# Dummy matmuls from the first microsecond, other banks for the last unit of the first group, and a few casts on other engines

## The chip, the cores and the metric

One Trainium2 chip, one of its cores. The metric is the device time of one execution in microseconds (us). The kernel before takes 340.81 us (median of 3 runs, 340.48 to 345.62). A difference counts as faster or slower from 2% on. A run is called slow when it is over 1.5% above the fastest of the same kernel (345.62 is one); fast runs are compared with fast runs.

## The reference, cut to what matters

```python
# retention: q, k, v of (8 batches, 8 heads, 576 positions, 64)
scores = scale * q @ k^T
ret = scores * Dmat          # Dmat = gamma_h ** (i - j) for i >= j, else 0
x = (ret @ v) -> (4608 tokens, 512)
# feed-forward with ELU
h = x @ w_in                 # 512 -> 2048
g = where(h > 0, h, exp(min(h, 0)) - 1)
out = g @ w_out              # 2048 -> 512
```

## The kernel before

The 4608 tokens go through the feed-forward in nine groups of 512. A group needs the attention output of some "units" (256 positions by four heads; unit 3 is the last that the first group waits for). For each unit VectorE and GpSimd scale q and k to bf16, TensorE transposes both, makes the scores, the running state (k times v) and the values (masked scores times v, plus q times the carried state), and ScalarE copies the result out of PSUM. GpSimd then writes the running state as a bf16 tile for TensorE; such a write is called a "state put" below. Meanwhile the weights arrive in fp32 by DMA and are cast to bf16. PSUM has three banks for `ps_h`, one for `ps_m`, two for the scores (`ps_s`), two for the values (`ps_x`).

The parts that the change touches (cuts are marked):

```python
    def warm(n, d=None):                       # dummy matmuls
        d = ps_s.tile([P, 2, 512], FP32, name="warm", tag="sc")[:, 0] if d is None else d
        for _ in range(n):
            mm(d, ident, zero, start=True, stop=True)

    def last_of_start(u):                      # unit 3, in two halves of two heads
        ...
        new_x()                                # the same two banks as unit 2's values
        both = [None]
        for hl in range(2):
            # VectorE: mask half hl of the scores
            if hl == 0:
                prefix_end(u)
                both.append([ps_h.tile([P, 512], FP32, name="o2", tag="ph") for _ in range(2)])
            values(u, (hl,), both[hl])
            inter(u, (hl,), both[hl])
            put_x(u, (hl,), both[hl], ("ss", "sv")[hl])
            warm(1, both[1][1] if hl == 0 else None)

    ...
    cast(0, "v", None)
    turn_pe(0)
    cast(1, "v", None)
    for u in range(FT - 1):
        scores(u)
        cast_v(u, "s")
        ...                                    # values of the unit before, states of this one
        if u == 2:
            cast_w(0)                          # two weight casts on GpSimd
            cast_v(3, "s")                     # unit 3's v on ScalarE
        ...
        masks(u)
        turn_pe(u + 1, "vs" if u == 2 else "ss")
        ...                                    # states of unit 3, sums, state puts, warm(1)
        if u == 1:
            cast_q(3, nc.vector)
            cast_q(3, nc.gpsimd, 1, (0,))      # unit 3's k: half on GpSimd,
            cast_q(3, nc.vector, 1, (1,))      # half on VectorE
    cast_w(1)
    scores(3)
    ...                                        # values of unit 2
    last_of_start(3)
    ...
    for ft in range(8):
        ffn1(0, ft, relu=ft % 2 == 1)          # four matmuls of 128x512, Exp (and Relu), one or two VectorE passes
    for ft in range(8):
        ffn1(0, 8 + ft, relu=ft % 2 == 1)
        ffn2(0, 0, [ft])
        ffn2(0, 1, [ft], ps_x, "x0")
```

## Time and profile before

| | before |
|---|---|
| time | 340.81 us (340.48 to 345.62) |
| profiled execution | 344.11 us, span 342.4 |
| first feed-forward matmul starts | 22.33 us |
| first copy of an output tile starts | 45.83 us |

The page gives each engine's busy share in 40 slices of the span (9 is 90% or more), and the TensorE clock that the throttle granted, in tenths:

```profile
PE   3889986678667899999999999999999999999995
PEclk9999999989899999999999999999999999999999
```

TensorE is busy for 90% or more of each slice from the 15th to the last but one. The first slices hold the start, and the clock row shows 9 there, although the matmuls run at half speed.

### The profile page before, as it was taken

To read this page: it belongs to the slowest core of one execution; us is meant where nothing else is said; L and a number is where in the kernel's file an instruction comes from. 1 tells how busy PE (TensorE), PEld (TensorE's weight loads), DVE (VectorE), ACT (ScalarE), POOL (GpSimd) and SP (SyncE) were. 2 spreads that over 40 slices of the span, in tenths; PEclk is the share of its full clock that TensorE was granted. 3 is DMA by queue.
4 is the path that set the end of the run, shared out by engine and by line. 5 is a ranking of instruction groups with operands and counts; after the bars stand their busy time and mean duration, and the time that the engine had idled before them with its cause. 6 is when DMAs were issued, how large, how long until landed. Compare 5 with 4: busy or idle time off the path is not lost.

```text
span 342.4 us, 7823 instructions
## 1 busy us (share of the span) xinstructions
PE 307.1 (90%) x3039; PEld 157.1 (46%) x3080; DVE 213.0 (62%) x379; ACT 178.8 (52%) x364; POOL 179.3 (52%) x315
## 2 busy tenths in 40 slices
PE   3889986678667899999999999999999999999995
PEld 1543434345444445444454544554454444444342
DVE  4838724566568998667676676677677565455500
ACT  3627612546244477655555565565556655555511
POOL 5789453555989479364565658556755120000100
PEclk9999999989899999999999999999999999999999
DMA  7999999203999979975259875978422001000021
GB/s 213 319 358 387 264 306 299 70 2 107 157 279 237 263 156 192 189 171 164 86 121 249 169 185 126 241 158 207 93 56 61 32 33 61 32 32 32 31 94 61
DMA packets 100293, 53.86 MB, mean 157 GB/s; under 512 B 44448, under 2 KB 93600, under 8 KB 100256
## 3 DMA queue, kind: packets, MB, share of 16 engines
q1 hardware_dynamic: 97696, 44.97, 55.5%
q0 software_dynamic: 2560, 8.39, 7.8%
q8 instruction: 24, 0.39, 0.5%
q14 instruction: 13, 0.11, 0.1%
HBM read 36.70 MB, written 9.44 MB: 135 GB/s over the span
## 4 chain that ended last, share of the span: by engine, by line
PE 78%; DVE 5%; DMA 5%; ACT 5%; POOL 3%; issue 3%; SPq 1%; DVEq 0%; ACTq 0%; POOLq 0%
PE ph L66 34%; PE pm L66 34%; PE x L66 5%; PE sc L66 3%; DMA qkT<-qkn 3%; DVE em L475 3%; DMA rqk<-in_k_dram 2%; POOL qkn L191 1%; DVE g L482 1%; ACT xt L343 1%; ACT ph L473 1%; ACT ot L492 1%; DVE g L480 1%; ACT e L471 1%; ACT qkT L240 1%
## 5 line engine op out<-in xcount | busy, mean ns | idle before, releaser
L66 PE MATMUL ph<-xt,w_in_sb 128*128 128x512 bf16 (+2 forms) x612 | 149.5, 366 | 10.4 <-DVE g L482 6.8
L66 PE MATMUL pm<-w_out_sb,g 128*128 128x512 bf16 x564 | 144.1, 380 | 2.9 <-ACT ot L492 1.7
L471 ACT ACTIVATE e<-ph 128x512 f32<-128x512 f32 (+2 forms) x152 | 87.3, 574 | 97.6 <-PE ph L66 79.7
L66 PEld LDWEIGHTS <-w_in_sb 128*128 128x128 bf16 x640 | 60.7, 100 | 72.4 <-issue 14.1
L66 PEld LDWEIGHTS <-g 128*128 128x128 bf16 x576 | 55.8, 98 | 69.6 <-issue 7.3
L480 DVE SCALAR_TENSOR_TENSOR g<-e,ph 128x512 bf16<-128x512 f32 (+2 forms) x80 | 50.2, 632 | 49.9 <-ACT ph L473 49.6
L475 DVE TENSOR_SCALAR em<-e 128x512 bf16<-128x512 f32 (+2 forms) x76 | 47.5, 625 | 32.2 <-ACT e L471 32.2
L495 POOL DMA_DIRECT2D out_dram<-ot x32 | 18.3, 573 | 81.5 <-ACT ot L492 81.5
L482 DVE SCALAR_TENSOR_TENSOR g<-ph,em 128x512 bf16<-128x512 f32 (+2 forms) x80 | 50.7, 637 | 3.4
L473 ACT ACTIVATE ph<-ph 128x512 f32<-128x512 f32 (+2 forms) x76 | 43.3, 570 | 0.0
L290 DVE TENSOR_TENSOR pt<-sc,mask 128x1024 bf16<-128x1024 f32 x31 | 37.7, 1217 | 6.8 <-PE sc L66 6.8
L191 POOL TENSOR_TENSOR qkn<-rqk,gk 128x256 bf16<-128x256 f32 x63 | 37.8, 618 | 3.6 <-DMA rqk<-in_k_dram 3.5
L343 ACT CAST xt<-x 128x256 bf16<-128x256 f32 (+1 forms) x72 | 24.2, 415 | 26.2 <-PE x L66 26.1
L492 ACT COPY ot<-pm 128x512 f32<-128x512 f32 x36 | 21.1, 589 | 20.1 <-PE pm L66 20.1
L191 POOL TENSOR_TENSOR qkn<-rqk,gq 128x256 bf16<-128x256 f32 x52 | 31.2, 620 | 0.1
L370 POOL TENSOR_TENSOR s_mid_146<-mid,diag 128x256 bf16<-128x256 f32 x16 | 9.7, 606 | 30.2 <-DVE mid L381 19.3
L370 POOL TENSOR_TENSOR s_mid_147<-mid,diag 128x256 bf16<-128x256 f32 x16 | 9.7, 609 | 28.7 <-DVE mid L381 14.4
L66 PE MATMUL sc<-qkT 64*64 64x128 bf16 (+1 forms) x576 | 16.8, 229 | 4.6 <-DMA qkT<-qkn 3.3
L217 POOL CAST vn<-rv 128x512 bf16<-128x512 f32 x27 | 17.9, 663 | 0.0
L239 PE MATMUL ptr<-ident,qkn 128*128 128x128 bf16 x64 | 8.5, 269 | 8.3 <-DVE qkn L191 6.1
L66 PEld LDWEIGHTS <-qkT 64*64 64x64 bf16 x576 | 10.5, 112 | 10.5 <-DMA qkT<-qkn 3.6
L66 PE MATMUL x<-pt,vn 64*64 64x128 bf16 x504 | 14.2, 227 | 0.5 <-ACT xt L343 0.5
(79 smaller groups left out, 183.2 us busy)
## 6 DMA issues: line engine op xcount, KB each, us to landing
rqk<-in_q_dram SPq DMA_DIRECT2D x32, 256.0 KB, 4.8
rqk<-in_k_dram SPq DMA_DIRECT2D x32, 256.0 KB, 4.6
rv<-in_v_dram SPq DMA_DIRECT2D x32, 256.0 KB, 4.9
out_dram<-ot POOLq DMA_DIRECT2D x32, 256.0 KB, 3.8
rqk<-in_moe_w_in_dram SPq DMA_DIRECT2D x16, 256.0 KB, 6.0
rqk<-in_moe_w_out_dram SPq DMA_DIRECT2D x16, 256.0 KB, 5.4
rqt<-in_q_dram SPq DMA_DIRECT2D x8, 128.0 KB, 4.4
rqt<-in_k_dram SPq DMA_DIRECT2D x8, 128.0 KB, 3.9
```

The costliest lines, as they stand in the source:

```text
L66: pin(nc.tensor.matmul(*a, **kw))
L191: pin(eng.tensor_tensor(natt[u][0][:, i, e], x[:, e], g[:, e], ALU.mult))
L290: pin(nc.vector.tensor_tensor(pt.rearrange("p i h n -> p (i h) n"), sc.rearrange("p i (h n) -> p (i h) n", h=2), mask.rearrange("p k e r - ...
L343: pin(engines[eng[c]](dst, src[:, :, :, a // 2 : (a + n) // 2]))
L370: pin(eng.tensor_tensor(dst.rearrange("p h (j d) -> p h j d", j=2), src.unsqueeze(2).to_broadcast([P, 2, 2, D]), diag.unsqueeze(1).unsquee ...
L471: pin(nc.scalar.activation(e[:, :m], ph[:, :m], AF.Exp))
L473: pin(nc.scalar.activation(ph[:, :m], ph[:, :m], AF.Relu))
L475: pin(nc.vector.tensor_scalar_add(em[:, :m], e[:, :m], -1.0))
L480: pin(nc.vector.scalar_tensor_tensor(dst, e[:, c], -1.0, ph[:, c], ALU.add, ALU.min))
L482: pin(nc.vector.scalar_tensor_tensor(dst, ph[:, c], 0.0, em[:, c], ALU.max, ALU.min))
L492: pin(nc.scalar.copy(ot, pm))
L495: pin(store.dma_start(out[i0 : i0 + P, :], ot))
```

## The change

The intent: keep TensorE busy from the start so that its clock is full when the feed-forward begins, and shorten the road to the first feed-forward matmul. The dummies use only the `zero` tile, so that they need not wait for the identity. Unit 3's values go into the banks that hold the states of units 3 and 2, so that they need not wait for unit 2's values to be copied out. Unit 3's k is now all on GpSimd, its v on GpSimd instead of ScalarE, and the first weight cast is on ScalarE.

```diff
     def warm(n, d=None):
-        d = ps_s.tile([P, 2, 512], FP32, name="warm", tag="sc")[:, 0] if d is None else d
+        d = xps[1] if d is None else d
         for _ in range(n):
-            mm(d, ident, zero, start=True, stop=True)
+            mm(d, zero[:, :P], zero, start=True, stop=True)
...
-    def last_of_start(u):
+    def last_of_start(u, banks):
...
-        new_x()
-        both = [None]
         for hl in range(2):
             ...
-            if hl == 0:
-                prefix_end(u)
-                both.append([ps_h.tile(...) for _ in range(2)])
-            values(u, (hl,), both[hl])
-            inter(u, (hl,), both[hl])
-            put_x(u, (hl,), both[hl], ("ss", "sv")[hl])
-            warm(1, both[1][1] if hl == 0 else None)
+            values(u, (hl,), banks[hl])
+            inter(u, (hl,), banks[hl])
+            put_x(u, (hl,), banks[hl], ("ss", "sv")[hl])
...
+    new_x()
+    warm(7)
     cast(0, "v", None)
-    turn_pe(0)
+    turn_pe(0, between=2)          # two dummies between the q and the k transposes
+    warm(2)
...
+        if u == 0:
+            ...                    # as before, and at its end
+            warm(2, st[1])
+        if u == 1:
+            ...
+            cast_q(3, nc.vector)
+            cast_q(3, nc.gpsimd, 1)
+            cast_v(3, "p")
+            warm(3, st[1])
+    cast_w(0, "s ")                # the first weight on ScalarE
+    masks(2)
+    turn_pe(3, "vs")
+    st3 = [ps_h.tile([P, TG], FP32, name="st", tag="ph") for _ in range(2)]
+    state(3, st3)
+    ...                            # the sums and puts of units 2 and 3, all before unit 3's masks
+    cast_w(0, " p")                # the second on GpSimd
     scores(3)
     ...
-    last_of_start(3)
-    prefix_end(2)
+    cast_w(1)
+    last_of_start(3, (st3, st))
```

More of the change, by code (lines that the diff above doesn't have):

```diff
@@ L151, in load_w, with cast_w @@
             pin(nc.sync.dma_start(staged[k][:, h], src))
-    def cast_w(k):
+    def cast_w(k, eng="pp"):
         for h, src, dst in weights(k):
-            pin(nc.gpsimd.tensor_copy(dst, staged[k][:, h]))
-        staged.pop(k)
+            if eng[h] != " ":
+                pin(engines[eng[h]](dst, staged[k][:, h]))
     rawt, natt, trt, ptt, score_ps, total = {}, {}, {}, {}, {}, {}
@@ L230, in turn, with turn_pe @@
             pin(nc.sync.dma_start_transpose(trt[u], flat(u)))
-    def turn_pe(u, eng="vs"):
+    def turn_pe(u, eng="vs", between=0):
         n = turn_tile(u)
         for i in range(2):
+            if i and between:
+                warm(between)
             if i * 4 < n:
@@ L413, in last_of_start @@
             ))
-            if hl == 0:
-                prefix_end(u)
-                both.append([ps_h.tile([P, 512], FP32, name="o2", tag="ph") for _ in range(2)])
-            values(u, (hl,), both[hl])
-            inter(u, (hl,), both[hl])
-            put_x(u, (hl,), both[hl], ("ss", "sv")[hl])
-            warm(1, both[1][1] if hl == 0 else None)
+            values(u, (hl,), banks[hl])
+            inter(u, (hl,), banks[hl])
+            put_x(u, (hl,), banks[hl], ("ss", "sv")[hl])
         drop(u)
@@ L531 @@
             drop(u - 1)
-        state(u, [ps_m.tile([P, TG], FP32, name="st", tag="pm"), ps_h.tile([P, TG], FP32, name="st", tag="ph")])
-        if u == 2:
-            cast_w(0)
-            cast_v(3, "s")
+        st = [ps_m.tile([P, TG], FP32, name="st", tag="pm"), ps_h.tile([P, TG], FP32, name="st", tag="ph")]
+        state(u, st)
+        if u == 0:
+            masks(0)
+            turn_pe(1, "ss")
+            prefix_mid(0)
+            prefix_end(0)
+            put_mid(0)
+            put_end(0)
+            cast(2, "v", None)
+            warm(2, st[1])
         if u == 1:
             cast(3, None, None)
-        masks(u)
-        turn_pe(u + 1, "vs" if u == 2 else "ss")
-        if u == 2:
-            state(3, [ps_h.tile([P, TG], FP32, name="st", tag="ph") for _ in range(2)])
-        prefix_mid(u)
-        put_mid(u)
-        if u == 2:
-            prefix_mid(3)
-            put_mid(3)
-        else:
-            prefix_end(u)
-            put_end(u)
-            warm(1)
-        if u == 0:
-            cast(2, "v", None)
-        if u == 1:
-            cast_q(3, nc.vector)
-            cast_q(3, nc.gpsimd, 1, (0,))
-            cast_q(3, nc.vector, 1, (1,))
-    cast_w(1)
+            masks(1)
+            turn_pe(2, "ss")
+            prefix_mid(1)
+            prefix_end(1)
+            put_mid(1)
+            put_end(1)
+            cast_q(3, nc.vector)
+            cast_q(3, nc.gpsimd, 1)
[6 more added lines that the diff above has]
+    state(3, st3)
+    prefix_mid(2)
+    put_mid(2)
+    prefix_end(2)
+    prefix_mid(3)
+    put_mid(3)
+    prefix_end(3)
+    cast_w(0, " p")
     scores(3)
```

## The prediction

> **What bounds the kernel now.** The page first: TensorE is busy in 90% of the span and carries 78% of the chain that ended last, but the 40 slices show its first ten partly below that (3889986678). The change touches only what stands before the first feed-forward group, so I read the chain of waits there, then the timeline, engine by engine. Chain (start, length, what):
>
> ```profile
> 18.22 1.17 PE x L66 x20
> 19.39 0.44 ACT xt L343
> 19.87 1.06 PE x L66 x9
> 20.93 0.36 issue
> 21.29 0.31 PE o_523 L66 x2
> ...
> 22.05 0.43 PE warm L66
> 22.47 3.44 PE ph L66 x8
> 25.96 0.47 issue
> ...
> 29.05 2.89 PE ph L66 x12
> ```
>
> Two things are to be seen. Unit 3 (the last of the first group) waits from 19.39 to 19.87 for ScalarE to copy unit 2 out of the same two banks, and only then do its matmuls, its copies and a dummy run, so the feed-forward starts at 22.33. And the first eight feed-forward matmuls take 3.44 us, 0.43 each. The same instruction is twice as fast later (TensorE's timeline; start, time, count):
>
> ```profile
> 22.33 5.30 PE L66 MATMUL ph<-xt,w_in_sb 128*128 128x512 bf16 x16
> ...
> 36.78 0.59 PE L66 MATMUL pm<-w_out_sb,g 128*128 128x512 bf16 x2
> 37.21 1.03 PE L66 MATMUL ph<-xt,w_in_sb 128*128 128x512 bf16 x4
> 38.08 0.59 PE L66 MATMUL pm<-w_out_sb,g 128*128 128x512 bf16 x2
> ```
>
> From 36.78 to 38.08 six matmuls start, 0.216 us each. The weight loads step by 0.43 us until 25.70 and by about 0.215 after it. So TensorE is at half speed for its first 25.8 us. The view of the granted clock prints 1.00 for these stretches, for its records begin only with the first change; the cadence is the evidence, not that column.
>
> What feeds unit 3 (timeline of all engines):
>
> ```profile
> 13.59 0.92 DVE L191 TENSOR_TENSOR qkn<-rqk,gq 128x256 bf16<-128x256 f32 x2 [0.56 <-DMA rqk<-in_q_dram]
> 14.52 0.61 POOL L191 TENSOR_TENSOR qkn<-rqk,gk 128x256 bf16<-128x256 f32 x1 [0.62 <-DMA rqk<-in_k_dram]
> 14.54 0.87 DVE L191 TENSOR_TENSOR qkn<-rqk,gk 128x256 bf16<-128x256 f32 x1
> 15.34 1.21 DVE L290 TENSOR_TENSOR pt<-sc,mask 128x1024 bf16<-128x1024 f32 x1
> 15.66 1.04 PE L239 MATMUL ptr<-ident,qkn 128*128 128x128 bf16 x8
> 16.73 0.59 ACT L240 COPY qkT<-ptr 128x512 bf16<-128x512 bf16 x1
> 18.26 0.69 DVE L410 TENSOR_TENSOR pt<-sc,mask 128x512 bf16<-128x512 f32 x1 [0.17 <-PE sc L66]
> 19.07 0.68 DVE L410 TENSOR_TENSOR pt<-sc,mask 128x512 bf16<-128x512 f32 x1
> ```
>
> Unit 3's q and k come from DMAs that land at about 13.6 and 14.5; the DMA engines are full from 4 us on (share 1.0 or more), and the change leaves their order alone. So nothing can move unit 3's k before 14.5. After that, 7.8 us pass until the feed-forward starts: casts, transposes, copy, states, scores, masks, values, copies.
>
> **What the Trainium skill says.** "TensorE: Matmul & The Clock Gate", Part 1 (The HAM clock gate): the array starts at half clock and is released after a busy window of about 3.4 us; the window is free-running, so the moment varies by run; a window of idle brings the half clock back. The trace agrees: 0.43 against 0.216 us, and full speed comes at 25.77, one window after dense 512-wide matmuls began at 22.33. It also shows that the small matmuls before did not do it: in 12.1 to 15.5 us I work out that columns streamed in some 74% of the time (a quarter of the window being transposes), and the clock stayed half. Part 4 (PE-mode transpose) states that transposes do not count as busy in the same way, which fits. Re-throttling is seen too: TensorE idles 1.97 us before 73.38, and from 73.56 the granted clock is 0.5 for 3.4 us; I work out 37% streaming in the window before. "Back-to-back issue gap" there gives 512/1.2 GHz = 427 ns cold for one dummy, as measured here.
>
> **The change, part by part.**
>
> *Dummies.* 16 added (7 at the start, 2+2 around unit 0's transposes, 2 after unit 0, 3 after unit 1), 4 removed. They now read only the zero tile, ready at 1.21 us, so seven run from about 1.25 to 1.25 + 7 x 0.427 = 4.24 us, where TensorE idled until 4.31 anyway: free. The next two fill 5.0 to 5.85 and push the k transposes from 5.39 by about 0.45, but the second k half is ready only at 5.96; cost 0 to 0.3 us in a stretch where units 1 to 3 wait for DMA. The others sit before scores that wait for ScalarE's copy. Their worth is the clock. Dense cover of a 3.4 us window is between 60% and 88% by phase, 80% or more with the transposes. The lowest window that I see release the clock is near 86 to 100%, the highest that fails is 74%, of which 25% transposes. I give 75% that the clock is full before 9 us, then some risk of losing it in 9 to 19 us, where warm matmuls stream only 30 to 50% of a window.
>
> *Road to the feed-forward, warm.* k of unit 3 lands at 14.45. Both halves are now on GpSimd, 14.52 + 2 x 0.61 = 15.74 (before 15.41, shared with VectorE): +0.3. VectorE, rid of its k half, does unit 2's mask at 14.51 instead of 15.34 and is free at 16.15 for copies and sums. Transposes end about 16.0 (before 16.70), ScalarE's copy at 16.05 to 16.65 (before 17.32); ScalarE's weight cast (0.6, about 15.3 to 15.9) just fits before it. GpSimd casts unit 3's v in 15.74 to 16.40 (0.66), so its states end near 16.9. VectorE's four sums take 0.39 each, 16.15 to 17.6; then unit 3's masks at 17.6 and 18.25, ending 18.3 and 18.95 (before 18.95 and 19.75). With its own banks the wait of 0.54 and the dummies fall away: values and carried part about 0.35, copies 0.45, twice, the second ending near 19.65. GpSimd is the rival on this road: the state puts until 17.86, then weights 1, 2, 3 at 0.57 each, until 19.57. So the start is about 19.8, against 22.33: **2.5 us**. Cold, the same road ends near 21.0 (scores, values and dummies at half speed): 1.3 us.
>
> *First eight feed-forward tiles.* Before, tile 0 starts at 22.33 and tile 8 at 31.96: 9.63. Warm, TensorE needs 8 x 4 x 0.216 = 6.9, but VectorE needs 4 x (0.61 + 0.69) + 4 x 0.69 = 8.0, and a tile waits for the product three tiles earlier (three banks). Walking that through, tile 8 starts after 7.4: **2.2 us**. Not the 8 x 0.215 = 1.7 of the cold matmuls alone, since the three banks then stay filled. Weights: tile 4 needs cast 7 (about 21.8; tile at 23.5), tile 8 needs cast 11 (25.3; 27.2), and the first w_out tile (28.2) would hold its matmuls some 0.2 us. **-0.2**.
>
> *After that* TensorE is the bound at 1.29 us a tile in both, and the order is the same to the end, so I expect the gain to be carried whole.
>
> Sum, warm: 2.5 + 2.2 - 0.2 = 4.5, so 336.3. Cold throughout: 1.3, so 339.5. Weighted 0.75 to 0.25: 337.1. The profiled run had its window begin just as the feed-forward did; an average run gets the clock up to a window later, so the change is worth about 0.5 more: **336.6**.
>
> **Rivals.**
> 1. *The clock is not released early, or lost again before the feed-forward.* For: no window before 22 us released it in the old kernel, and windows at 37% lost it. Against: windows at 38% and 41% near 53 to 63 us kept it. Time: 338 to 339.5.
> 2. *GpSimd's casts take over as the bound.* It does 0.57 to 0.66 us pieces without a pause from 14.5 to 38. For: weight 3 is done 0.2 us before I need it. Against: one cast moved to ScalarE and the weights land (w3 at 17.25) well before. If it slips by 0.6, 337.2.
> 3. *A transfer or a later wait eats the gain.* w_out's last half lands at 38.1 whatever happens; but it is needed only near 41. The inputs for the next group land at 39 to 48 and are used from 48 on, so 4.5 us earlier still holds. Time if lost: 340.
> 4. *More gain.* The start cannot come before about 19.2 (DMA at 14.45 and the chain behind it), the first eight tiles cannot gain over 2.5; with a late clock in the old kernel's runs 6.5 in all: 334.3.
>
> **Range and chances.** 334.4 to 339.6 holds the warm case with an error of 1.5 to 2 us and the cold case. Faster by over 2% needs under 334.0, a gain of 6.8, more than rival 4 can collect: 0.06. Slower by over 2% has no mechanism: 0.01. Runs with a lost clock window (the old kernel's 345.62, the profiled 344.11) are of another state and are not the comparison.
>
> **What would show it.** Dummies from about 1.25 us; the dummies after unit 0 at 0.216 us a piece and not 0.43; unit 3's masks ending near 18.9 and its values following without ScalarE's wait; the first feed-forward matmul at 19.8 (19.3 to 20.5); tile 8 starting 7.4 us after it; about 4.5 us less at the first output copy (45.83 before). Wrong if the matmuls at 20 us still step by 0.43, if GpSimd's weight cast ends the wait before the first feed-forward matmul, or if the first output copy is early and the end is not.

## The result, and the profile after

The changed kernel takes 337.03 us (median of 4 runs, 335.59 to 338.07); the old one beside it takes 340.84 (4 runs). The ratio is 0.9889, with a 95% interval of 0.9843 to 0.9935: the same within 2%, and clear of no change. A ratio is the mean time of one kernel's fast runs over that of the other's fast runs of the same rounds, so it is not quite the ratio of the medians. The profiled run of the changed kernel was its fastest, 335.59 us, with a span of 333.9. Its two rows of the slices:

```profile
PE   7789985767679999999999999999999999999995
PEclk9999999999979999999999999999999999999999
```

In the first slice TensorE is now busy for 7 tenths instead of 3; that is the dummies. The timeline of all engines, start and length in us, of the lines that answer to those shown of before:

```profile
1.27 3.17 PE L66 MATMUL x<-zero 128*128 128x512 bf16 x7 [1.27 <-DVE zero L75]
...
14.65 1.21 DVE L292 TENSOR_TENSOR pt<-sc,mask 128x1024 bf16<-128x1024 f32 x1
14.74 1.19 POOL L191 TENSOR_TENSOR qkn<-rqk,gk 128x256 bf16<-128x256 f32 x2 [0.62 <-DMA rqk<-in_k_dram]
...
15.66 0.63 ACT L156 CAST w_in_sb<-rqk 128x512 bf16<-128x512 f32 x1
...
16.31 0.59 ACT L242 COPY qkT<-ptr 128x512 bf16<-128x512 bf16 x1
...
17.89 1.28 DVE L410 TENSOR_TENSOR pt<-sc,mask 128x512 bf16<-128x512 f32 x2
...
18.62 0.31 PE L66 MATMUL st<-pt,vn 64*64 64x128 bf16 x8 [0.46 <-DVE pt L410]
...
19.58 2.75 PE L66 MATMUL ph<-xt,w_in_sb 128*128 128x512 bf16 x11
...
20.20 1.85 PEld L66 LDWEIGHTS <-w_in_sb 128*128 128x128 bf16 x10 [0.30 <-POOL w_in_sb L156]
```

The dummies start at 1.27. Unit 3's k lands late as before (GpSimd starts at 14.74, waiting for the DMA), VectorE masks unit 2 at 14.65 instead of 15.34, unit 3's values wait for VectorE's mask and no longer for ScalarE, and the first feed-forward matmul starts at 19.58 instead of 22.33. Eleven of them span 2.75 us, so they run at the full clock; the record of the clock has the release at 4.74. The weight loads stop 0.30 us before 20.20 for a weight cast of GpSimd, but the matmuls keep their step of 0.216 us through it (twelve slots from 19.58 to 22.17, with one record missing), so the start of the feed-forward doesn't wait for it. The chain of waits (start, length, what) says what holds the stretch after it:

```profile
17.72 0.61 POOL s_mid_147 L372
18.33 4.10 POOL w_in_sb L156 x7
22.43 0.58 POOL s_end_149 L372
23.01 0.57 POOL s_end_151 L372
23.58 5.04 POOL w_in_sb L156 x8
28.62 0.57 POOL w_out_sb L156
29.19 0.04 issue
29.23 0.59 PE pm L66 x2
...
42.17 0.60 ACT ot L488
```

Before, this stretch was TensorE, at half clock, and VectorE. Now the chain names GpSimd's state puts and casts, one after the other, until the first matmul with w_out at 29.23. The first output copy starts at 42.17, against 45.83: 3.66 us earlier.

The next table follows the difference to the end, from the timelines of several profiles. The last column has the stretches of half clock that the record of the clock shows after the first release and before 110 us, by their start; each is one window of 3.41 us, except where a number of windows is given.

| profile | first ff matmul | first output copy | from there to the 4th | 4th to 6th | 6th to last | half clock from |
|---|---|---|---|---|---|---|
| before (slow run) | 22.33 | 45.83 | 15.28 | 47.22 | 230.23 | 73.6, 90.6 |
| before, again (state unknown) | 22.70 | 46.21 | 16.34 | 48.15 | 227.11 | 57.4, 91.5, 108.6 |
| changed | 19.58 | 42.17 | 15.29 | 46.18 | 226.38 | 93.5 |
| changed, again | 19.84 | 42.40 | 16.58 | 48.86 | 226.39 | 9.7, 54.1, 95.1 (3) |
| no dummies (e2) | 20.62 | 43.87 | 15.28 | 45.52 | 226.60 | 91.6 |
| more dummies (e6) | 19.26 | 41.74 | 15.29 | 46.69 | 226.38 | 69.4, 93.3 |

The gain is made before the first output copy and is not given back. What scatters the time afterwards lies almost all before 110 us: the stretch from the first to the fourth output copy takes 1.1 to 1.3 us more when a half-clock window falls in it (16.34 and 16.58 against 15.28). From the sixth copy on the changed kernels need 226.4 to 226.6 us in every profile of this table. Part of the scatter of the first column is the landing of unit 3's k, which differs from profile to profile: 14.45 in the old kernel's first, 14.77 in its second, 14.67 in the changed one's, 14.28 in e6's. The old kernel's slow profile has 230.23 there; it holds a single stop of TensorE of 3.69 us before 112.85 that the other profile of that kernel lacks (112.85 is after its sixth copy, at 108.33), so its span of 342.4 is not to be held against 333.9.

### The profile page after: what moved, and what is told of

It is laid out like the page before. It is cut to its first block, busy times and chain, and to the rows that moved or that the text cites.

```text
span 333.9 us, 7841 instructions
## 1 busy us (share of the span) xinstructions
PE 303.7 (91%) x3049; PEld 154.4 (46%) x3092; DVE 208.1 (62%) x378; ACT 178.8 (54%) x364; POOL 180.7 (54%) x316
## 4 chain that ended last, share of the span: by engine, by line
PE 76%; POOL 9%; DVE 4%; DMA 3%; ACT 3%; issue 2%; SPq 0%; POOLq 0%; ACTq 0%; DVEq 0%
PE pm L66 35%; PE ph L66 32%; PE x L66 5%; PE sc L66 3%; POOL qkn L191 3%; POOL w_in_sb L156 3%; DMA qkT<-qkn 2%; DMA rqk<-in_q_dram 2%; DVE pt L292 1%; DVE g L478 1%; ACT ot L488 1%; DVE em L471 1%; POOL s_mid_147 L372 1%; ACT xt L345 1%; ACT ph L469 1%
## 5 line engine op out<-in xcount | busy, mean ns | idle before, releaser
L66 PE MATMUL ph<-xt,w_in_sb 128*128 128x512 bf16 (+2 forms) x611 | 145.7, 358 | 6.6 <-DVE g L478 3.7
L66 PEld LDWEIGHTS <-w_in_sb 128*128 128x128 bf16 x640 | 59.3, 98 | 66.2 <-issue 8.0
L471 DVE TENSOR_SCALAR em<-e 128x512 bf16<-128x512 f32 (+2 forms) x76 | 43.2, 569 | 31.4 <-ACT e L467 31.4
L191 POOL TENSOR_TENSOR qkn<-rqk,gk 128x256 bf16<-128x256 f32 x64 | 38.5, 621 | 3.5 <-DMA rqk<-in_k_dram 3.5
L66 PE MATMUL sc<-qkT 64*64 64x128 bf16 (+1 forms) x576 | 16.1, 222 | 3.2 <-DMA qkT<-qkn 2.8
L217 POOL CAST vn<-rv 128x512 bf16<-128x512 f32 x28 | 18.8, 671 | 0.0
L66 PE MATMUL x<-pt,vn 64*64 64x128 bf16 x496 | 13.1, 221 | 0.0
L241 PE MATMUL ptr<-ident,qkn 128*128 128x128 bf16 x64 | 7.3, 227 | 5.7 <-POOL qkn L191 2.3
```

Source lines behind the costliest of these rows:

```text
L66: pin(nc.tensor.matmul(*a, **kw))
L191: pin(eng.tensor_tensor(natt[u][0][:, i, e], x[:, e], g[:, e], ALU.mult))
L217: pin(engines[eng](natt[u][1], rawt[u][1]))
L471: pin(nc.vector.tensor_scalar_add(em[:, :m], e[:, :m], -1.0))
```

## The experiments

Eleven runs, of ten kernels and the old one again, were made. All were correct. The old kernel took 339.3 to 340.3 us (medians) beside them. The first two calls ran on one chip, the third (e7, e8, e9) on another, so means are compared within the first two or within the third, and ratios across them.

### e1: the dummies alone

The old kernel with the new `warm`, `new_x(); warm(7)`, `between=2`, `warm(2)`, `warm(2, st[1])` and `warm(3, st[1])`; nothing else of the change.

> The old kernel with the new dummies alone (seven from 1.25 us on, two and two around unit 0's transposes, two after unit 0, three after unit 1; the two in its last unit stay), nothing else moved. Theory (the clock brings most of the gain): full clock by about 5 us, first feed-forward matmul near 20.3 us instead of 22.33, steps of 0.216 us there, time about 337.5 (ratio to the old kernel 0.990). Rival (the rearrangement brings most of it, the clock little, because the road to the feed-forward waits for DMA, GpSimd and VectorE): feed-forward still after 21.3, about 339.5 (0.996).

Measured: 338.49 us, ratio 0.9968 (0.9932 to 1.0005). The clock was released at 4.87 us, as expected, and lost again for two windows from 18.53, so the feed-forward, from 21.75 on, ran its first matmuls at half clock and the first output copy came at 45.20. Neither theory had that: the dummies won the clock and did not hold it. Alone they are worth about 1 us, an amount that the interval does not tell from nothing.

### e2: the change without its dummies

```diff
-    warm(7)
...
-    turn_pe(0, between=2)
-    warm(2)
+    turn_pe(0)
...
-            warm(2, st[1])
...
-            warm(3, st[1])
```

> The changed kernel without any of its 16 dummies; banks, casts and order as changed. Theory: half clock until one window after the feed-forward begins; matmuls step by 0.43 us there; first feed-forward matmul near 21.0 us; time about 339.5 (ratio to the old kernel 0.996). Rival (rearrangement brings most): first feed-forward matmul near 20 us and about 337.5 (0.990).

Measured: 339.45 us (336.63 to 340.50), ratio 0.9973 (0.9924 to 1.0021). The profile has the half clock until 23.3 us, the first feed-forward matmul at 20.62 and the first output copy at 43.87. The theory's time holds in the median; the six runs fall into two groups (336.6 and 336.8, four at 339.0 to 340.5), and the profile is of one of the two quick ones. In that trace the rearrangement alone brings the first output copy 2.0 us forward (45.83 to 43.87), more than the 1.3 that I had given it, and already the first feed-forward matmul comes 1.7 us earlier. The two parts alone sum to 0.6% and the whole change has 0.9 to 1.1%; with intervals of about 0.4% on each side this does not tell whether the parts help each other.

### e3: the end-state puts behind the weight casts

```diff
     cast_w(3)
-    put_end(2)
-    put_end(3)
     cast_w(4)
...
         cast_w(kk)
+    put_end(2)
+    put_end(3)
     load_to(FT + 7)
```

> The changed kernel with the two end-state puts of GpSimd (2 x 0.57 us in front of the third block of weight casts) moved behind all weight casts. Theory A (GpSimd's chain of casts holds the first w_out matmul by 0.44 us, at 29.23, and nothing else): that wait goes, the first w_out matmul starts at about 28.8, time 0.4 us less than the changed kernel's 337.0, so about 336.6. Theory B (GpSimd's chain bounds the whole stretch from 18.3 to 29.2, as the chain of waits paints it): its 1.15 us come off in full, about 335.9. Theory C (DMA, VectorE and ScalarE hold it just as long): no change.

Measured: 336.52 us (335.08 to 337.94), ratio 0.9899 (0.9857 to 0.9941); the change itself has 0.9889 and 0.9911 in its two sets of runs. So no change in the time that these runs can tell; theory B, 1.15 us in full, has no support. In this profile the first w_out cast is at 28.03 (28.57 in the changed kernel) although the feed-forward began a microsecond later, and the first w_out matmul comes at 31.06, far after it: GpSimd was then not the bound. The run showed something else (chain of waits):

```profile
16.80 0.62 ACT w_in_sb L156
17.42 0.49 ACT qkT L242
```

The first weight landed at 16.78 here (15.35 in the profile of the changed kernel), and ScalarE, whose program has the cast before unit 3's transposed copy, stood idle 0.85 us for it and came to that copy only at 17.32 by its timeline (16.31 in the changed kernel's). The first feed-forward matmul came at 20.63, at half clock, for the clock had been lost at 10.29 and again at 20.53.

### b0: the kernel before, once more

> The old kernel once more, for a profile in the fast state. If lost clock windows make the slow state, its time is about 340.7, the trace has at most one stretch of half clock between 26 us and the end, and its full clock begins 3.4 to 6.8 us after the first feed-forward matmul at about 22.3 us.

Measured: 343.36 us, one run, of unknown state; span 341.6. The clock was released at 26.66, 3.96 us after the first feed-forward matmul at 22.70, as expected. But the trace has three windows of half clock after that, and of 11 runs of this kernel, those at the lower times do not all have the higher clock (338.71 us at 0.993, 338.93 at 0.980). My expectation of one window and 340.7 us was wrong; the granted clock of a run does not order the times.

### a1: the changed kernel again

> The changed kernel once more, beside the others of this call. Theory (the clock, won by about 5 to 7 us, is lost again in some runs because the small matmuls of units 1 to 3 fill too little of a window): the time scatters over 335.5 to 338, with a ratio to the old kernel near 0.989; the profile shows full clock from 4.7 to 8 us on and, in some three cases of four, a stretch of half clock before 24 us, and then a first output copy at about 43.5 to 44 us instead of 42.2. Rival (the clock is kept and the scatter comes from later): no half clock before 24 us.

Measured: 336.88 us (335.81 to 339.81), ratio 0.9911 (0.987 to 0.9952). The theory of a clock that is won and lost holds: released at 6.33, lost at 9.74, back at 13.16. It came back before the feed-forward, so the cost was small: first output copy at 42.40, where I had expected 43.5 or more. TensorE's busy time by window of the clock (window, its length, busy time and count of matmuls, printed clock, DMA share, GB/s):

```profile
6.33:9.74 3.41, 2.21 (x43) 1.00 1.20 305
9.74:13.16 3.42, 3.06 (x59) 0.50 1.21 294
13.16:16.57 3.41, 2.92 (x65) 1.00 1.03 349
16.57:19.98 3.41, 2.46 (x73) 1.00 1.05 390
```

(The last window ended with the clock kept.) The window before the loss has 2.21 us of busy records in 3.41; the later ones, which kept the clock or won it, have more. Over all profiles, seven windows of the start ended in a loss of the clock: in six of them busy time was 1.69 to 2.21 us, in the seventh 2.39. Of the windows of the start that kept it in the profiles that I read so, one had 2.08, the others 2.30 or more. Records of matmuls can be missing, so this is no sharp border, but "fills too little of the window" is borne out. Counting columns instead of busy time orders them better. An estimate from the records' starts (0.216 us for 512 columns at the full clock; a 64x64 matmul as a quarter, since four start within 0.01 us) gives 25 to 32% of the window for the seven that lost the clock and 34% or more for all that kept it before 22 us, the one with 2.08 included (41%); 32 and 34 lie so near that missing records could close the gap. Later windows give no border: in the same part of the program a1 kept the clock with 1.49 us busy (67.77 to 71.18) and e6 lost it with 1.45 (65.99 to 69.41), both at 35% by this count.

### e4: unit 3 back in unit 2's banks

```diff
         ptt[u] = pt
+        new_x()
+        banks = (None, banks[0])
         for hl in range(2):
```

> The changed kernel with the last unit's matmuls put back into the two banks of unit 2 (first half) and two fresh ones (second half): the first half waits for ScalarE to copy unit 2 out again. Theory: the wait of some 0.5 us is back, the first feed-forward matmul comes 0.3 to 0.5 us later and so does the end. Rival (GpSimd's weight casts hold the feed-forward's first tile anyway, since weight 3 was cast 0.1 to 0.3 us before it was needed): no change.

Measured: 337.00 us (335.92 to 339.22), ratio 0.9931 (0.9886 to 0.9976), against 0.9911 for the change (means 337.19 and 337.26): not to be told apart by the time. The wait is back in the timeline of this kernel:

```profile
18.72 0.61 PE L66 MATMUL x<-pt,vn 64*64 64x128 bf16 x8 [0.53 <-ACT xt L345]
...
19.26 0.29 PE L66 MATMUL x<-qkT,s_end 128*128 128x128 bf16 x1
```

and the second of these matmuls in the changed kernel's:

```profile
18.86 0.23 PE L66 MATMUL st<-qkT,s_end_150 128*128 128x128 bf16 x1
```

VectorE's masks start at 17.91 here and at 17.89 there, and both had the full clock up to 19.20, just before that matmul. So the old banks cost 0.40 us on the road in this pair of profiles, as theory had it; the rest of the 0.53 lies beside the mask. After 19.20 this profile is at half clock, so its first feed-forward matmul (20.56) cannot be held against 19.58. GpSimd had cast weight 3 by about 20, so the rival, that the casts hold the first tile anyway, is not seen.

### e5: the first weight cast on GpSimd

```diff
-    cast_w(0, "s ")
...
-    cast_w(0, " p")
+    cast_w(0)
```

> The changed kernel with the first weight cast back on GpSimd, none on ScalarE. Theory: GpSimd's chain of casts gets 0.57 us longer in front of the first tile, which then starts about 0.4 us later; the first w_out matmul too (0.5 us later than 29.23 in the same clock state); time +0.4 to 0.5. Rival: ScalarE's cast stands ahead of unit 3's transposed copy in a queue that goes in order, and where the first weight lands late (16.8 us in one run) it holds that copy by 0.6; then taking it away costs nothing or gains up to 0.3.

Measured: 337.39 us (336.69 to 337.73), ratio 0.9928 (0.9893 to 0.9963), against 0.9911. The profile can be compared with that of a1, since both lost the clock in the same windows (9.9 and 9.7, 54). The first feed-forward matmul is at 19.64 against 19.84, the first w_out matmul at 29.82 against 29.47, the first output copy at 42.76 against 42.40. So the longer chain on GpSimd costs 0.36 us at the first output in this pair of profiles, near what theory had, but not at the first tile. It is below what the time can show.

### e6: seven more dummies where TensorE idled

```diff
-            turn_pe(1, "ss")
+            turn_pe(1, "ss", between=2)
...
+    warm(2, st3[0])
     state(3, st3)
...
+            warm(2 - hl, banks[hl][1])
             values(u, (hl,), banks[hl])
```

> The changed kernel with 7 more dummies where TensorE idled: two between unit 1's transposes (8.8 us), two before unit 3's states (16.3), two and one before the halves of its values (18.2, 19.0). Theory (windows that stream under about 40% lose the clock): the clock holds from its first release to the group after, in nearly all runs; first output copy near 42.2 us; time 1 us under the changed kernel in the mean, with less scatter. Rival (the dummies stand in the road, or the clock is not lost by lack of activity): same time or up to 0.6 us more.

Measured: 335.91 us (335.67 to 336.98), ratio 0.9893 (0.9857 to 0.9928), against 0.9911 for the change. The mean of its six runs is 336.13 with a standard deviation of 0.5; the change has 337.26 and 1.3. The profile has no half clock between 4.55 and 69.4 us, the first feed-forward matmul at 19.26 and the first output copy at 41.74. That first matmul comes 0.32 us earlier than in the changed kernel's profile, but unit 3's k landed 0.39 us earlier too, so the dummies didn't shorten the road. By window of the clock (here with the columns of all engines; TensorE's is the first):

```profile
7.96:11.38 3.42, 2.91 (x60) 1.45 (x62) 3.10 (x6) 1.76 (x4) 3.20 (x5) 1.00 1.22 291
11.38:14.79 3.41, 2.68 (x68) 1.66 (x65) 2.60 (x6) 2.40 (x6) 2.30 (x5) 1.00 1.13 333
14.79:18.20 3.41, 2.75 (x62) 1.45 (x61) 2.60 (x8) 1.98 (x6) 2.76 (x6) 1.00 1.05 371
```

Each is at 2.68 us or above; the window before them, 4.55 to 7.96, has 2.63. The theory's 1 us is what the means show (337.26 - 336.13), but with a scatter of 1.3 over six runs it is not settled by the time alone; that none of the three profiles with these seven (e6, e7, e8) lost the clock before 54 us, while five of the six with the change's dummies from the start (the two of the change, e1, e3, e4, e5) did so before 24, carries more.

### e7: these, the weight cast behind the copy, and the puts behind

```diff
-    cast_w(0, "s ")
     masks(2)
     turn_pe(3, "vs")
+    cast_w(0, "s ")
```

and the diffs of e3 and e6.

> The changed kernel with the 7 more dummies of the run before, ScalarE's weight cast moved behind unit 3's transposed copy, and the two end-state puts behind all weight casts. Theory: the copy no longer waits for a late first weight (16.8 us in one run), so the first feed-forward matmul stays at 19.2 to 19.6 in every run, GpSimd's chain is 1.15 us shorter, first output copy near 41.7; mean 0.2 to 0.5 us under the kernel with the dummies alone (336.1). Rival (the first eight tiles are held by VectorE and ScalarE, and the DMA gap was rare): same as that kernel within 0.2 us.

Measured: 335.81 us (335.30 to 337.03), ratio 0.9882 (0.9857 to 0.9908). Its ratio is 0.0011 under that of e6, with intervals of 0.0025 and more on each side, so the rival holds within what can be told. The first weight landed late in its profile too (16.33), and ScalarE copied unit 3 at 16.84, before it cast the weight at 17.32: the hold-up is gone. Yet the first feed-forward matmul came at 20.18, not at 19.2 to 19.6: unit 3's k landed at 14.96, GpSimd cast it until 16.46 (until 15.93 in the changed kernel), and VectorE's masks of unit 3 began at 18.42 instead of 17.89. The chain up to the first w_out matmul, at 29.44, is DMAs of w_in and then GpSimd's casts. This is the lowest median of all the kernels, 1.2% under the old one by its ratio; over the change the gain is about 1 us, and not settled.

### e8: dummies in the second group too

```diff
+    fill = {9: (0, 2), 10: (0, 4), 11: (3, 2), 12: (5, 3)}
     def scores(u):
         ...
+        warm(fill.get(u, (0, 0))[1], sc[:, 0])
...
         new_x()
+        warm(fill.get(u, (0, 0))[0])
         if late:
...
+        if ft == 9:
+            warm(5, ps_s.tile([P, 2, 512], FP32, name="warm", tag="sc")[:, 0])
         ffn1(1, ft, 0, 320, relu=ft % 2 == 1)
```

on top of e7.

> The kernel before this one and dummies in the idle stretches of the second group too (5 near 68 us, 2 to 8 in each of four units between 78 and 93 us). Theory (what scatters the time after 50 us is the clock lost in windows near 54, 70 and 94 us, each worth up to 1.7 us): fewer stretches of half clock between 50 and 110 us, granted clock 0.993 or more in most runs, time 0.5 to 1.5 us less. Rival (those windows wait for VectorE, GpSimd and DMA at any clock, and dummies stand in the way): same or up to 1 us more.

Measured: 336.69 us (336.03 to 337.61), ratio 0.991 (0.9887 to 0.9932). The clock did what the theory wanted: 0.988 to 0.995 in the six runs, and in the profile no half clock between 57.7 us and the end stretch, where every other profile has a window lost between 86 and 98. The time is 0.8 us worse than that of e7 in the means. From the fourth to the sixth output copy it takes 46.06 us, and e7, with a lost window at 95.0, takes 45.82. So the rival is right about the time. The trace still shows TensorE stopped there at the full clock, 0.82 us before 93.63 for a DMA transpose and 0.35 before 87.80 for a state put. Whether the full clock gains nothing there, or gains what the new dummies cost, no run separates.

### e9: without the first seven

```diff
     new_x()
-    warm(7)
```

> The changed kernel without the seven dummies from 1.25 us; the other nine stay. Theory (the dense 3 us at the start are what releases the clock): no full clock before 20 us, first feed-forward matmul at about 20.6 to 21, time like the kernel without any dummy, 338.9 in its mean. Rival (the nine around units 0 and 1 do it as well, with the transposes): full clock from some 8 to 11 us on in most runs, time within 0.5 us of the changed kernel.

Measured: 338.34 us (335.85 to 338.93), ratio 0.9939 (0.9906 to 0.9972). The clock was full at 7.98 us: the nine others around units 0 and 1 released it as well in this profile, as the rival had it, and my theory that it takes the first seven falls. In this profile it was lost at 18.22 for one window. By the ratios, 0.9939 against 0.9911, it is about 0.9 us behind the change, with intervals of over 0.003 on each side; the rival had put it within 0.5. So the first seven are not needed to win the clock, and what they are worth beyond that is not settled.

## Why the prediction was right or wrong

The time is right: 336.6 predicted, 337.03 measured, inside the range, and within 2%. By its steps:

- **Dummies free, clock early.** Right. The first starts at 1.27 us (1.25 predicted). In all nine profiles with the seven dummies the clock was full between 4.55 and 6.88 us; I had given 75% for "before 9 us".
- **"Some risk of losing it in 9 to 19 us".** This was much more than some risk: it was lost before 24 us in five of the six profiles with just the change's dummies. Rival 1 was thus right in what happens and wrong in its price. Where the loss falls at 9.7 us it costs the first output only 0.2 us (42.40 against 42.17, with unit 3's k landing at 14.66 and 14.67); where it reaches the feed-forward the first output is later (45.20 in e1, 44.06 in e3, though each has another cause as well).
- **Road to the feed-forward.** 19.8 predicted, 19.58 and 19.84 in the two profiles of the change. The pieces are where they were put: the mask of unit 2 at 14.65 (14.51 predicted), the copy of the transposed k at 16.31 (16.05), unit 3's masks at 17.89 (17.6). The road without the clock was predicted to end near 21.0 and ends at 20.62 (e2). The sum behind 17.6 was wrong in two sizes that nearly cancel: VectorE's four sums take about 0.30 us each, not 0.39, and it waits 0.56 us for unit 3's states before 17.28. The new banks are worth 0.4 us of the road (e4). No run takes away the moves of unit 3's k and v alone; what they are worth is read from the lines, not tested.
- **First eight tiles: the step that failed.** A tile is four matmuls, 128x512 of h, counted from 0. I had tile 8 start 7.4 us after tile 0; it starts at 27.93, 8.35 after 19.58. So this term is 9.63 - 8.35 = 1.3 us, not 2.2. The walk took VectorE's passes one after the other, with 0.61 us for the subtraction. The timeline, of TensorE and of VectorE:

```profile
22.74 3.94 PE L66 MATMUL ph<-xt,w_in_sb 128*128 128x512 bf16 x16 [0.41 <-DVE g L478]
27.07 1.24 PE L66 MATMUL ph<-xt,w_in_sb 128*128 128x512 bf16 x5 [0.38 <-DVE g L478]
...
24.92 0.69 DVE L476 SCALAR_TENSOR_TENSOR g<-e,ph 128x512 bf16<-128x512 f32 x1 [0.33 <-ACT ph L469]
```

The 32 matmuls need 6.9 us at 0.216; the other 1.45 are four stops between matmul slots. The two long ones, 0.57 before 22.74 and 0.55 before 27.07, are waits for VectorE to free a bank (the view counts 0.41 and 0.38, since it adds the modelled end of a matmul); 0.18 and 0.16 fall before 24.64 and 25.66. That VectorE paces this stretch was right; its passes were sized too short. The subtraction takes 0.63 to 0.77 us here, and VectorE waits 0.33 us for ScalarE's Relu before 24.92, which the sum had left out.
- **Weights.** The wait for the first w_out tile is 0.44 us (28.79, the end of tile 8's four slots of 0.216, to 29.23), predicted 0.2. Rival 2 is right to that extent: GpSimd is the chain from 17.7 to 29.2 in the profile. But taking 1.15 us from it (e3) changed no time that the runs can tell; that VectorE and ScalarE hold the same stretch nearly as long is my reading of the waits above, not shown by a run.
- **The sum.** 2.75 + 1.28 - 0.44 = 3.6 against 3.66 measured at the first output copy, and against 4.5 predicted for the warm case. The predicted time was near partly by luck: the mix with the cold case took 0.8 back. It was meant for a clock never won, and what stands in its place is the slower tiles and a clock lost again.
- **Carried whole.** Right: from the first to the fourth output copy 15.29 us against 15.28, to the sixth 46.18 against 47.22, and no more after that than before.
- **The 0.5 us for a late clock in the old kernel's runs** is neither shown nor refuted: one more profile of it had the clock 3.96 us after its first feed-forward matmul, against 3.44 in the first.

## What to carry to other kernels

Dummy matmuls won TensorE's full clock here by 4.55 to 6.88 us, but with the small matmuls after them it was lost again in five of six profiles, so fill the later gaps as well, up to the dense stage; look at several profiles, since the windows fall differently in each run. Ask what the others wait for before paying for a full clock: here it brought 1.7 us at the first output copy (43.87 without dummies, 42.17 with them and the clock kept), and e8 shows no gain in a stretch where TensorE waits for state puts and transposes. A weight cast ahead of an urgent copy in an engine's program holds that copy when the weight lands late (in e3 until 17.32, against 16.31).

## What the Trainium skill lacked or had wrong

- "TensorE: Matmul & The Clock Gate", Part 1 (The HAM clock gate), speaks of an idle window that brings the half clock back, and of frequent short idles that do so, with no share of busy time. Here, at the start, windows were enough in which TensorE was busy by the records for 1.69 to 2.21 of 3.41 us (one of 2.39), and windows of 2.30 and more kept it, with one exception at 2.08. After 50 us windows of 1.5 us kept it too (a1, 67.77 to 71.18), so these runs give no number for the page either.
- The same part gives a busy window as what releases the clock. In the old kernel a window with 3.10 of 3.41 us busy by the records (12.12 to 15.53) did not release it; much of it is transposes and 64x64 matmuls. Part 4 there says that transposes do not count in the same way; that fits, but it does not explain the case: in e3 a window at half clock with as much (3.12 us, 10.29 to 13.70, and 1.03 us of it transposes against 1.04) did release the clock, as did 3.06 us in a1 (9.74 to 13.16). These followed a window at the full clock; whether that matters no run shows.
- No page says whether matmuls of zeros by zeros release the clock. With the seven dummies and unit 0's transposes it was released in nine of nine profiles, at 4.55 to 6.88 us.
- No page says that the record of the granted clock can print full speed before its first event: 1.00 is printed while matmuls step by 0.43 us instead of 0.216.
